# A hashed attention with a max-out network on one core: an earlier projection, a shorter run of zero products, and weights, quad projection and one hash at other units

## The chip, the cores and the metric

The kernel runs on one core of one Trainium2 chip. The metric is device time in microseconds, the median of several executions. TensorE is called PE in the profile, VectorE DVE, ScalarE ACT, GpSimd POOL, and SyncE SP. PE's weight loads are listed apart as PEld.

## The reference

Two stages follow each other. Only the first output feeds the second:

```python
# q, k, v: (4, 8, 768, 64) float32; proj: (64, 6)
q_bits = (einsum('bhsd,dk->bhsk', q, proj) > 0)      # 6 hash bits for each query
k_bits = (einsum('bhsd,dk->bhsk', k, proj) > 0)      # 6 hash bits for each key
mask   = bucket(q_bits)[..., :, None] == bucket(k_bits)[..., None, :]
scores = where(mask, q @ k.T / 8, -1e9)
attn   = softmax(scores)
x      = (attn @ v).transpose(0, 2, 1, 3).reshape(3072, 512)
h      = maximum(maximum(x @ w1, x @ w2), x @ w3)    # w1..w3: (512, 768)
out    = h @ w_out                                    # (768, 512)
```

## The kernel before

The hash bits are appended to the queries and keys as extra rows (plus and minus a half), so that one matrix product gives the scores and the comparison of the buckets together. A *unit* is one set of score products (L296, function `scores`), 768 score columns in all, followed by one exponential on ACT (L304) into an `AT` tile. There are 192 units, 48 for each of the four batches (`UPB`). The first batch is cut into chunks of 256 queries and the others into chunks of 384. Within the first three chunks the heads come in the order 0, 1, then 2 and 3, then 4 to 7; in later batches a batch's chunk runs through its eight heads, so that heads 4 to 7 of the second batch start at unit 60. `scores(u + 1)` is issued at the head of the loop body of unit `u`.

Queries and keys must stand with the 64 dimensions on the partitions. The first batch's heads 0 to 7 of both sides are grouped in *pairs* (0 to 3, two heads each). They are loaded in natural order (`load_pair`, L117), transposed on PE with the identity (`pair_turn`, L122), copied out of PSUM by DVE or ACT (`pair_keep`, L129 and L131), and narrowed into the tile `S` by POOL (`pair_place`, L136). The bits are products with the small projection `pj2` (L149, L169), compared with zero by DVE (L152, L174). The other batches are grouped in *quads* of four heads (`g` from 2 to 7, `g = 3` being heads 4 to 7 of the second batch): loaded by SP or POOL (`load_quad`, L194), transposed in blocks on DVE (`turn`, L200), narrowed by POOL (`narrow`, L205), placed into `S` by DMAs of SP (`place`, L210), and hashed by `quad_hash`: eight pairs of PE products with the quad projection `pj` (L219), one comparison on DVE (L222), and four DMAs of SP that put the bits into `S` (L230).

The order on every engine is the order of the program text (a manual schedule). Before the loop stand the first loads, a run of products of the tile `warm`, which is zero (L498), and the first pair's transposes, hash and placement. Both projections come from the same small tile `pst`, the projection matrix loaded by one DMA (L478): `pj2` is filled by two copies on DVE and two on POOL (L493), `pj` by a memset and four copies on POOL (L534, L536). The values come by `load_v` (L238) and the weights of the network by `load_weights` (L246, and L243 for the output weights), all through POOL's queue.

Other steps are attached to units by `when(u, f)`: they run in the body of unit `u`, behind `scores(u + 1)`. Then come one or two groups of the network (`ffn_groups`: L406 products, L411, L413 or L415 evacuation; L450 products and L454 copy for the output), then the *burst* of a finished set of four heads, if one is due (`burst`: sums of the exponentials, L351, and values, L373). A quad's hash is the last thing in its unit, and its four DMAs are put at the head of the next:

```python
            if u in hash_at:
                when(u + 1, quad_hash(hash_at[u]))
```

The PSUM banks other than those of the scores are four, given out and returned in program order.

Of the kernel before, what the change touches and what calls it, by code (L numbers as in the profile page):

```python
# [17 lines left out]
def kernel(  # L18
# [12 lines left out]
    nc = tc.nc  # L31
    B, H, S, D = q.shape
    NBITS = proj.shape[1]
# [7 lines left out]
    Q = 32  # L41
# [35 lines left out]
    pj = konst.tile([P, 2, Q], FP32, name="pj")  # L77
    pj2 = konst.tile([P, Q], FP32, name="pj2")
    pst = konst.tile([Q, 2, NBITS], FP32, name="pst")
# [10 lines left out]
    def bank():  # L90
        i = free_banks.pop(0)
        return i, bank_tiles[i]
# [7 lines left out]
    def start_set(name, heads):  # L100
        nat[name] = nat_pool.tile([P, 4 * NM * D], FP32, tag="nat", name="nat")
        for x, key in enumerate(heads):
            where[key] = (name, x)
# [7 lines left out]
    def load_pair(pi, eng, sides=(1, 0), h0=0, h1=2):  # L111
        if pi not in nat:
            start_set(pi, [(0, 2 * pi), (0, 2 * pi + 1), (1, 2 * pi), (1, 2 * pi + 1)])
        n = nat[pi].rearrange("p (s h w) -> p s h w", s=2, h=2)
        for side in sides:
            src = (q, k)[side][0, 2 * pi + h0 : 2 * pi + h1].rearrange("h (p c) d -> p h (c d)", p=P)
            eng.dma_start(n[:, side, h0:h1, :], src)  # L117
# [15 lines left out]
    def pair_place(pi, side, par, h0=0, h1=2):  # L133
        o = s_tile(pi)[0:D, 2 * side + h0 : 2 * side + h1, par * HALF : (par + 1) * HALF]
        i_ = t32[pi][par * D : (par + 1) * D, side, h0 * HALF : h1 * HALF].rearrange("d (h n) -> d h n", n=HALF)
        nc.gpsimd.tensor_scalar(out=o, in0=i_, scalar1=RS, scalar2=1.0, op0=AluOp.mult, op1=AluOp.mult)  # L136
# [98 lines left out]
    def load_v(g):  # L235
        b, h0 = divmod(4 * g, H)
        t = v_at[g] = vo_pool.tile([P, 4, NM * D], FP16, tag="vo", name="vo")
        nc.gpsimd.dma_start(t[:], v[b, h0 : h0 + 4].rearrange("h (p c) d -> p h (c d)", p=P))  # L238


    def load_weights(i):
        if i == 3:
            nc.gpsimd.dma_start(wout_sb[:], moe_w_out.rearrange("(c p) f -> p c f", p=P))  # L243
            return
        w = (moe_w1, moe_w2, moe_w3)[i]
        nc.gpsimd.dma_start(w_sb[i].rearrange("p (i u) f -> p i (u f)", u=2),  # L246
                            w.rearrange("(i p u) f -> p i (u f)", p=P, u=2))
# [224 lines left out]
    def when(u, f, *args):  # L472
        at.setdefault(u, []).append(lambda: f(*args))

    with tc.manual_schedule():
        load_pair(0, nc.sync, (1,), 0, 1)
        load_pair(0, nc.scalar, (0,), 0, 1)
        nc.sync.dma_start(pst[:], proj.rearrange("(u d) k -> d u k", d=Q))  # L478
        nc.vector.memset(warm[:], 0.0)
        make_identity(nc, iden[:])  # L480
        load_pair(0, nc.sync, (1,), 1, 2)
# [9 lines left out]
        for hd in range(2):  # L491
            for u in range(2):
                (nc.vector, nc.gpsimd)[hd].tensor_copy(  # L493
                    pj2[hd * D + u * Q : hd * D + (u + 1) * Q, hd : hd + 2 * NBITS - 1 : 2], pst[:, u, :])
        load_v(0)
        iw, wp = bank()
        for n in range(11):
            nc.tensor.matmul(wp[:, 0:HALF], warm[:, 0:P], warm[:], start=True, stop=True)  # L498
        give(iw)

# [30 lines left out]
        for side in (1, 0):  # L531
            for par in range(2):
                pair_place(0, side, par, 1, 2)
        nc.gpsimd.memset(pj[:], 0.0)  # L534
        for x in range(4):
            nc.gpsimd.tensor_copy(pj[x * Q : (x + 1) * Q, :, x : x + 4 * NBITS - 3 : 4], pst[:])  # L536

        for pi, us in ((1, ((0, 1, 0), (0, 0, 0), (3, 1, 1), (4, 0, 1))), (2, ((6, 1, 0), (7, 1, 1), (9, 0, 0), (10, 0, 1))),
                       (3, ((11, 1, 0), (13, 1, 1), (14, 0, 0), (15, 0, 1)))):
            for u, side, hd in us:  # L540
                when(u, pair_group, pi, side, hd, nc.scalar if pi == 1 and hd == 1 else None)
                if pi == 1:
                    for par in range(2):
                        when(u, pair_place, pi, side, par, hd, hd + 1)
                elif hd == 1:
                    for par in range(2):
                        when(u, pair_place, pi, side, par)
# [7 lines left out]
        when(18, pair_hash, 3)  # L555
        when(19, t32.pop, 3)
        when(17, load_v, 1)
        for n, u in ((0, 3), (1, 12), (2, 21), (3, 31)):
            when(u, load_weights, n)
        when(13, load_quad, 0, 2, range(4), nc.gpsimd)  # L560
        for u, side, g in ((23, 1, 3), (27, 0, 3)):
# [1 line left out]
        hash_at = {}  # L563
        for g in range(2, NQUAD):
            b2, i2 = divmod(g, 2)
            need = UPB * b2 + 12 * i2
            for n, side in enumerate((1, 0)):
                name = (side, g)
                if g > 3:
                    us = [SPREAD[b2][0] + SPREAD[b2][1] * (8 * i2 + 4 * n + n2) // 4 for n2 in range(4)]  # L570
                    for x in range(4):
                        when(us[0] - 14 + x, load_quad, side, g, (x,), nc.gpsimd)
                else:
                    us = [need - {2: 26, 3: 23}[g] + 4 * n + n2 for n2 in range(4)]
                for n2, u2 in enumerate(us):
                    when(u2, turn, name, n2 // 2, n2 % 2)
                    if n2 % 2:
                        when(u2 + 1, narrow, name, n2 // 2)
                when(us[3] + 3, place, name, range(4))
            hash_at[{2: 32, 3: 48, 4: need - 12}.get(g, need - 9)] = g  # L580
            when({2: 36, 3: 46}.get(g, need - 22), load_v, g)

        ffn, credit = [], 0
# [2 lines left out]
        for c, i in sorted(done_at, key=lambda e: done_at[e]):  # L586
            d = done_at[c, i] + LAG[c > 2]
            sums, values = burst(c, i)
            pieces = [lambda f=sums: f(0, NM), lambda f=values: f(0, 0, NM), lambda f=values: f(1, 0, NM)]
            for n, f in enumerate(pieces):  # L590
                u = {(0, 0): (16, 17, 20), (1, 0): (21, 22, 24), (2, 0): (26, 27, 29)}.get((c, i), (d, d, d))[n]
# [67 lines left out]
```

## Time and profile before

| | |
|---|---|
| median of 3 runs | 268.19 us (267.94 to 268.28) |
| the profiled execution's own time | 268.58 us |
| its span, first to last instruction | 266.6 us |
| PE busy | 257.9 us (97%) |
| DVE busy | 208.9 us (78%) |
| ACT busy | 177.3 us (67%) |
| POOL busy | 69.9 us (26%) |
| DMA | 30.95 MB, mean 116 GB/s |

The times of the rows of a trace count from the start of the span. The profiled execution is one execution, 0.39 us above the median of the others, and 1.98 us of its time lie outside its span. In rows of the timeline, the first number is the start, the second the duration, and `x3` says that three instructions are merged in the row. Bracketed is the idle time of the engine ahead of the row and what ended it, as far as the profile can tell. SPq, ACTq and PEldq are the queues that issue. The pages name a tile by the name that the program gave it, and both projections `pj` and `pj2` go by `pj` there.

### The profile page before, as it was taken

What the parts mean: (1) busy time and instruction counts of PE and PEld (TensorE: products, weight loads), DVE (VectorE), ACT (ScalarE), POOL (GpSimd) and SP (SyncE); (2) the same over time, 40 slices, a digit from 0 to 9 for tenths busy, and PEclk for the clock granted to TensorE, in tenths of its full rate; (3) what the DMA queues carried; (4) which work ended last, traced back from release to release, by engine and by line L of the source; (5) the groups of instructions that cost most, each with busy time, mean ns of one, the idle gap of its engine ahead of it and who ended that gap; (6) DMA issues with size and microseconds to landing.
All of it is one profiled execution on the core that took longest, in us unless ns stands there. A gap on an engine that the chain in (4) does not pass through costs nothing.

```text
span 266.6 us, 6482 instructions
## 1 busy us (share of the span) xinstructions
PE 257.9 (97%) x2505; PEld 154.4 (58%) x2505; DVE 208.9 (78%) x493; ACT 177.3 (67%) x257; POOL 69.9 (26%) x132
## 2 busy tenths in 40 slices
PE   7899999999799999999999999999999999999995
PEld 4555557885566575555555554555555555554552
DVE  2897685987499999978998997899849785888361
ACT  3596785676758694984869578484895859581322
POOL 3588652355032535240141612011000000000000
PEclk9999999999999999999999999999999999999999
DMA  6977999969703791982054472802030003000303
GB/s 203 316 156 135 230 234 212 245 114 233 185 22 86 159 231 18 234 222 53 4 167 131 56 182 43 204 8 61 15 118 4 0 2 119 2 0 2 118 0 118
DMA packets 20717, 30.95 MB, mean 116 GB/s; under 512 B 2608, under 2 KB 15248, under 8 KB 20688
## 3 DMA queue, kind: packets, MB, share of 16 engines
q0 software_dynamic: 8128, 13.37, 26.6%
q1 hardware_dynamic: 12128, 16.66, 21.8%
q10 hardware_dynamic: 432, 0.52, 0.6%
q8 instruction: 19, 0.31, 0.5%
q14 instruction: 10, 0.08, 0.1%
HBM read 25.17 MB, written 6.29 MB: 118 GB/s over the span
## 4 chain that ended last, share of the span: by engine, by line
PE 84%; DVE 7%; ACT 5%; issue 3%; DVEq 0%; ACTq 0%
PE ms L406 31%; PE sc L296 21%; PE ms L373 11%; PE ms L450 10%; ACT AT L304 4%; PE ms L351 3%; PE ms L219 3%; DVE ht L415 2%; DVE ad L327 1%; PE ms L498 1%; PE ms L122 1%; PE ms L149 1%; DVE T L131 1%; PE ms L169 1%; DVE S L174 1%
## 5 line engine op out<-in xcount | busy, mean ns | idle before, releaser
L304 ACT ACTIVATE AT<-sc 128x768 f16<-128x768 f32 x192 | 152.3, 816 | 62.2 <-PE sc L296 60.7
L406 PE MATMUL ms<-xT,w_sb 128*128 128x384 f16 (+1 forms) x648 | 114.8, 307 | 0.1
L296 PE MATMUL sc<-S 72*128 72x384 bf16 (+1 forms) x432 | 93.6, 308 | 3.3 <-ACT AT L304 1.8
L406 PEld LDWEIGHTS <-w_sb 128*128 128x128 f16 x648 | 62.7, 97 | 35.9 <-issue 0.4
L415 DVE TENSOR_TENSOR ht<-ht,ms 128x384 f16<-128x384 f16 (+1 forms) x108 | 54.3, 504 | 24.4 <-PE ms L406 13.4
L296 PEld LDWEIGHTS <-S 72*128 72x128 bf16 (+1 forms) x432 | 39.4, 98 | 35.7 <-issue 15.5
L205 POOL TENSOR_SCALAR T<-T 128x768 bf16<-128x768 f32 x24 | 22.8, 952 | 95.4 <-issue 50.5
L450 PE MATMUL ms<-wout_sb,ht 128*128 128x512 f16 x138 | 35.5, 378 | 0.0
L373 PE MATMUL ms<-AT,vo 128*32 128x385 f16 (+3 forms) x864 | 35.2, 309 | 0.3 <-DVE ht L415 0.3
L327 DVE TENSOR_TENSOR ad<-ad,AT 128x768 f16<-128x768 f16 x48 | 26.6, 553 | 2.1 <-ACT AT L304 1.3
L373 PEld LDWEIGHTS <-vo 128*32 128x32 f16 x864 | 22.6, 96 | 9.6 <-issue 1.8
L200 DVE STREAM_TRANSPOSE T<-nat 128x384 f32<-128x384 f32 x48 | 27.0, 565 | 0.2 <-DMA nat<-in_q_dram 0.2
L327 DVE TENSOR_TENSOR ad<-AT,AT 128x768 f16<-128x768 f16 x48 | 26.2, 546 | 0.2 <-ACT AT L304 0.2
L411 ACT CAST ht<-ms 128x384 f16<-128x384 f32 x36 | 17.3, 479 | 8.1 <-PE ms L406 8.1
L380 DVE SCALAR_TENSOR_TENSOR xT<-ms,sv,rb 128x384 f16<-128x384 f32 (+1 forms) x36 | 19.8, 567 | 1.4
L450 PEld LDWEIGHTS <-ht 128*128 128x128 f16 x138 | 13.3, 97 | 13.0 <-issue 0.3
L454 ACT COPY osb<-ms 128x512 f32<-128x512 f32 x21 | 12.2, 585 | 8.2 <-PE ms L450 6.3
L330 DVE TENSOR_TENSOR ad<-ad 128x384 f16<-128x384 f16 x32 | 15.5, 484 | 1.1
L136 POOL TENSOR_SCALAR S<-T 64x384 bf16<-64x384 f32 (+1 forms) x23 | 14.2, 617 | 5.0 <-DVE T L131 3.5
L358 DVE STREAM_TRANSPOSE ys<-ms 128x384 f32<-128x384 f32 (+1 forms) x18 | 9.6, 532 | 6.2 <-PE ms L351 6.2
L194 POOL DMA_DIRECT2D nat<-in_q_dram x20 | 11.1, 560 | 0.1
L413 DVE CAST ht<-ms 128x256 f16<-128x256 f32 x18 | 7.4, 413 | 4.0 <-PE ms L406 3.9
(48 smaller groups left out, 123.0 us busy)
## 6 DMA issues: line engine op xcount, KB each, us to landing
out_dram<-osb SPq DMA_DIRECT2D x21, 256.0 KB
S<-T SPq DMA_DIRECT2D x48, 96.0 KB
nat<-in_q_dram POOLq DMA_DIRECT2D x20, 192.0 KB, 6.7
vo<-in_v_dram POOLq DMA_DIRECT2D x8, 384.0 KB, 6.2
nat<-in_k_dram POOLq DMA_DIRECT2D x16, 192.0 KB, 5.7
w_sb<-in_moe_w_dram POOLq DMA_DIRECT2D x3, 768.0 KB, 6.9
nat<-in_k_dram SPq DMA_DIRECT2D x10, 192.0 KB
nat<-in_k_dram SPq DMA_DIRECT2D x3, 384.0 KB
```

The source lines that it names most:

```text
L200: nc.vector.transpose(t32[name][:, u, half * HALF : (half + 1) * HALF], i_)
L205: nc.gpsimd.tensor_scalar(out=t16[name][:, u, :], in0=t32[name][:, u, :], scalar1=RS, scalar2=1.0, op0=AluOp.mult, op1=AluOp.mult)
L296: nc.tensor.matmul(views[j], s_of[kn][0 : D + bits, kx, m * P : (m + 1) * P], s_of[qn][0 : D + bits, qx, q0 : q0 + w], start=True, stop=True)
L304: nc.scalar.activation(t[:, :, 0:w], whole, ActFn.Exp, bias=-SCALE * 0.25 * bits, scale=SCALE)
L327: nc.vector.tensor_tensor(out=sum_of[c, h][:], in0=t[0], in1=t[n], op=AluOp.add)
L330: nc.vector.tensor_tensor(out=t[:, 0, :], in0=t[:, 0, :], in1=t[:, 1, :], op=AluOp.add)
L373: nc.tensor.matmul(av[Q * x : Q * (x + 1), 0:n], v_at[2 * b + i][:, x, cb * D + side : (cb + 1) * D : 2], weights_of(c, 4 * i + x, m)[:, 0 ...
L380: nc.vector.scalar_tensor_tensor(out=xt_of(c)[:, 2 * i + side, 0:w], in0=av[:, 0:w], scalar=sv_of[b, i, side][:], in1=rb[0][:, 0:w], op0=A ...
L406: nc.tensor.matmul(ps[:, 0:w], w_sb[wi][:, jc, fb * P : (fb + 1) * P], xt[:, jc, 0:w], start=(jc == 0), stop=(jc == NJC - 1))
L411: nc.scalar.copy(hts[fb][:, 0:w], ps[:, 0:w])
L415: nc.vector.tensor_tensor(out=hts[fb][:, 0:w], in0=hts[fb][:, 0:w], in1=ps[:, 0:w], op=AluOp.max)
L450: nc.tensor.matmul(ps[:, 0:DM], hts[fb][:, tb * P : (tb + 1) * P], wout_sb[:, fb, :], start=(fb == 0), stop=(fb == NFB - 1))
```

## The change

The projection's load moves from SP's queue to the head of ACT's queue, ahead of the first queries. The run of zero products is cut from eleven to nine. The first weight is issued right behind the first values, ahead of the loop, instead of at unit 3; the second at unit 9 instead of 12, the third at unit 20 instead of 21. The quad projection `pj` is filled at unit 19 instead of ahead of the loop. The hash of quad 3 is put at unit 47 instead of 48.

```diff
     with tc.manual_schedule():
         load_pair(0, nc.sync, (1,), 0, 1)
+        nc.scalar.dma_start(pst[:], proj.rearrange("(u d) k -> d u k", d=Q))
         load_pair(0, nc.scalar, (0,), 0, 1)
-        nc.sync.dma_start(pst[:], proj.rearrange("(u d) k -> d u k", d=Q))
...
         load_v(0)
+        load_weights(0)
         iw, wp = bank()
-        for n in range(11):
+        for n in range(9):
             nc.tensor.matmul(wp[:, 0:HALF], warm[:, 0:P], warm[:], start=True, stop=True)
...
-        nc.gpsimd.memset(pj[:], 0.0)
-        for x in range(4):
-            nc.gpsimd.tensor_copy(pj[x * Q : (x + 1) * Q, :, x : x + 4 * NBITS - 3 : 4], pst[:])
-
+        def fill_pj():
+            nc.gpsimd.memset(pj[:], 0.0)
+            for x in range(4):
+                nc.gpsimd.tensor_copy(pj[x * Q : (x + 1) * Q, :, x : x + 4 * NBITS - 3 : 4], pst[:])
+
+        when(19, fill_pj)
...
-        for n, u in ((0, 3), (1, 12), (2, 21), (3, 31)):
+        for n, u in ((1, 9), (2, 20), (3, 31)):
             when(u, load_weights, n)
...
-            hash_at[{2: 32, 3: 48, 4: need - 12}.get(g, need - 9)] = g
+            hash_at[{2: 32, 3: 47, 4: need - 12}.get(g, need - 9)] = g
```

## The prediction

> **What bounds the kernel now.** First the head of the page: busy time by engine and the chain that ended last.
>
> ```profile
> span 266.6 us, 6482 instructions
> PE 257.9 (97%) x2505; PEld 154.4 (58%) x2505; DVE 208.9 (78%) x493; ACT 177.3 (67%) x257; POOL 69.9 (26%) x132
> PE 84%; DVE 7%; ACT 5%; issue 3%; DVEq 0%; ACTq 0%
> ```
>
> TensorE (PE) is busy for 257.9 of 266.6 us and carries 84% of the chain. So the time is the sum of PE's work plus its gaps, 8.7 us in all, and a change gains what it takes out of either, if nothing late takes its place. I then read the timeline where PE is not dense. The first place is the start. Columns: start, duration, engine, line, operation; in brackets the idle time before it and what ended it.
>
> ```profile
> 0.74 0.89 ACTq L117 DMA_DIRECT2D nat<-in_q_dram  x2
> 1.13 3.70 PE L498 MATMUL ms<-warm 128*128 128x384 f16 x11 [1.13 <-DVE pj L487]
> 1.19 0.42 SPq L478 DMA_DIRECT2D pst<-in_proj_dram  x1
> 4.01 0.37 SPq L117 DMA_DIRECT2D nat<-in_q_dram  x1
> 4.29 0.34 DVE L493 COPY pj<-pst 32x6 f32<-32x6 f32 x2 [2.68 <-DMA pst<-in_proj_dram]
> 4.62 1.10 PE L122 MATMUL ms<-iden,nat 128*128 128x128 f32 x6
> 4.95 0.95 POOL L238 DMA_DIRECT2D vo<-in_v_dram  x1 [0.18 <-issue]
> 5.44 0.56 DVE L131 COPY T<-ms 128x384 f32<-128x384 f32 x1 [0.81 <-PE ms L122]
> 6.05 1.44 PE L169 MATMUL ms<-T,pj 128*6 128x384 f32 x8 [0.32 <-DVE T L131]
> 6.09 1.57 POOL L136 TENSOR_SCALAR S<-T 64x384 bf16<-64x384 f32 x3 [0.20 <-DVE T L131]
> 6.90 2.31 DVE L174 TENSOR_SCALAR S<-ms 6x384 bf16<-6x384 f32 x4 [0.90 <-PE ms L169]
> 8.08 0.49 PE L296 MATMUL sc<-S 70*128 70x256 bf16 x3 [0.60 <-DVE S L174]
> 9.09 1.48 PE L122 MATMUL ms<-iden,nat 128*128 128x128 f32 x12
> ```
>
> The first transposes (L122, 4.62) show no wait: they stand behind eleven products of zeros (L498), and all after them is a chain: T copy on DVE (5.44), hash on PE (6.05), bits on DVE (6.90), first scores (8.08). Whoever starts the transposes earlier moves that chain.
>
> The second place is one unit of the scores, far behind the start:
>
> ```profile
> 56.67 0.60 PE L406 MATMUL ms<-xT,w_sb 128*128 128x256 f16 x4
> 57.10 0.49 PE L296 MATMUL sc<-S 72*128 72x384 bf16 x2
> 59.95 1.46 PE L219 MATMUL ms<-T,pj 128*32 128x384 f32 x16
> 61.49 0.56 DVE L222 TENSOR_SCALAR bits<-ms 128x384 bf16<-128x384 f32 x1 [0.28 <-PE ms L219]
> 53.29 6.18 SPq L210 DMA_DIRECT2D S<-T  x8
> 62.08 2.94 SPq L230 DMA_DIRECT2D S<-bits  x4
> 69.54 0.49 PE L296 MATMUL sc<-S 72*128 72x384 bf16 x2
> 69.87 0.60 PE L406 MATMUL ms<-xT,w_sb 128*128 128x256 f16 x4
> 71.95 0.48 PE L296 MATMUL sc<-S 72*128 72x384 bf16 x2 [1.48 <-ACT AT L304]
> 72.91 0.42 DVE L415 TENSOR_TENSOR ht<-ht,ms 128x256 f16<-128x256 f16 x1 [1.89 <-PE ms L406]
> L304 ACT ACTIVATE AT<-sc x60: 804/811/854, 8.6 to 70.1; 128x768 f16<-128x768 f32 x60
> PE sc L296 <- ACT AT L304: 1.5, 1, 1.5
> ```
>
> PE stands still for 1.48 us before the scores at 71.95. The last two lines are the instructions of L304 up to 71.9 us (count, then nanoseconds) and the waits of PE between 60 and 84 us. Sixty units had been activated by then, so the scores that wait are unit 60's: the first of heads 4 to 7 of the second batch (48 units a batch, 12 for the first four heads), the quad g = 3. The profile names ACT as releaser, but the last activation started at 70.1 and took 0.81, so it was done at 70.95, a whole microsecond earlier. What unit 60 alone needs are the hash bits of quad 3. They are hashed at 59.95, written by DVE until 62.05, sent by SP in four DMAs from 62.08 to 65.02. Busy time and DMA load by stretch (the last three columns are PE clock, DMA share, GB/s):
>
> ```profile
> 58.00:72.00 14.00, 12.52 (x150) 8.07 (x150) 8.75 (x21) 9.17 (x13) 4.44 (x16) 1.00 1.03 212
> 72.00:74.00 2.00, 2.00 (x16) 1.49 (x17) 1.09 (x3) 1.47 (x2) 0.00 (x0) 1.00 0.06 14
> ```
>
> The DMA engines are full from 58 on (share 1.03) and nearly empty right after 72 (0.06): the bits came with the last of that load. For comparison, quad 2's four sends and the scores that use them, which did not wait:
>
> ```profile
> 48.37 2.96 SPq L230 DMA_DIRECT2D S<-bits  x4
> 56.34 0.49 PE L296 MATMUL sc<-S 72*128 72x384 bf16 x2
> ```
>
> There 7.97 us from the first send were enough; in quad 3's case 9.87 (62.08 to 71.95) passed.
>
> **The change, part by part.** *Two zero products fewer.* From the first of eleven to the transposes behind the last it is 4.62 - 1.13 = 3.49 us, so they are 0.32 apart, and two are 0.64. The transposes could start at 3.98. They also need the first keys. SP's issue at 4.01 is the seventh there; a wait of 0.4 us stands before it in the list of SP's waits:
>
> ```profile
> SPq L117 <- DMA nat<-in_q_dram: 0.4, 1, 0.4
> ```
>
> So the first queries had landed at about 4.0; of the keys, issued on SP ahead of the projection's 1.19, no row shows it. They are there by 4.62; nearest is the queries' 4.0. That bounds this gain by 0 and 0.64. I take 0.5, near the upper end, since the keys go out as early as the queries.
>
> *The projection ahead of the queries on ACT's queue.* One issue costs 0.42 (SP's row at 1.19). It leaves SP, whose later loads go out 0.45 earlier, and puts the queries back by 0.42, to 4.4. They are needed after the three transposes of the keys (half of 1.10 behind 4.0 to 4.1, so 4.55): hidden by 0.1; beyond that the bits of the queries, second in the row of four at 6.90, give another half microsecond of cover. The projection itself, issued at 0.74 for 1.19, lands about 0.45 earlier, 3.84 for 4.29, so its two DVE copies (0.34) are over at 4.2, ahead of the T copy due at 4.9. Cost nothing.
>
> *First weight behind the first values.* POOL now issues it ahead of three placements (6.09, 1.57). Its issue is 0.76:
>
> ```profile
> 17.06 0.76 POOL L246 DMA_DIRECT2D w_sb<-in_moe_w_dram  x1
> 12.68 0.93 POOL L536 COPY pj<-pst 32x12 f32<-32x12 f32 x4
> 33.66 0.82 POOL L205 TENSOR_SCALAR T<-T 128x768 bf16<-128x768 f32 x1 [2.50 <-DVE T L200]
> ```
>
> POOL's values issue ended at 5.90; 0.45 earlier that is 5.45, and with the weight 6.21. The placements then run 6.21 to 7.78, the first over at 6.73 against first scores due at 8.08 - 0.5 = 7.6. Hidden by 0.8. The 0.76 at 17.06 and the quad projection's copies at 12.68 leave a POOL that nobody waits for there; nothing gained. The quad projection at unit 19 is queued ahead of the narrowing at 33.66, where POOL idled 2.50: 0.93 and a memset fit. Second weight three units, third one unit earlier: nothing on the path.
>
> *Hash of quad 3 at unit 47 instead of 48.* It now stands behind the feed-forward group at 56.67, where the scores at 57.10 began, so 59.95 - 57.10 = 2.85 us earlier. PE's work is only reordered: the scores at 57.10 and the sums and values between them and 59.95 go back by the hash's 1.4 us and end where the hash ended. DVE's bits end 2.10 us after the hash starts (62.05 - 59.95), now at 59.2. On SP they stand behind the eight placements (53.29 + 6.18 = 59.47), so the first send goes at 59.5 for 62.08: 2.6 us earlier. If landing follows, unit 60's data are there at 71.92 - 2.6 = 69.3, and even at the 9.87 us of that crowded stretch at 69.4. PE would come to unit 60 one step of 0.77 after 69.54 (groups of scores and L406 stand at 69.54 and 69.87), at 70.31. So the wait goes with about 0.9 to spare. What it is worth: 1.48 (gap) to 1.64 (71.95 - 70.31); I take 1.48. Late next is ACT, done with unit 59 at 70.95 and needed by unit 61's scores at 71.1; then DVE, which had idled 1.89 for the same stall and so moves with PE.
>
> **Sum.** 0.5 + 1.48 = 1.98 us off the profiled execution's 268.58 gives 266.6; that execution was 0.39 above the median of 268.19. Against the median: 266.2.
>
> **The rivals.** (a) *The bits land earlier, but not enough.* They follow 8 placements in one SP queue while the DMA engines are full; half of the 2.6 us would put them at 70.6, leaving 0.3, a quarter at 71.3, leaving about 1. Time 266.5 to 267.2. Against it: those values' end, which POOL's next quad loads are queued behind, also comes 1.4 us later, so they press on the bits later. (b) *The stall is not the bits*, and stays: only 0.5 is won, 267.7. For it: no row names the DMA. Against it: quad 3's first unit is the one that waits, and 0.06 of DMA share right after.
>
> (c) *The clock opens later.* The products of zeros have 384 columns and go 0.32 apart; two scores of 384 columns fill 69.54 to 69.87, 0.165 each. So PE starts at half rate, though the granted clock reads 1.00 in every stretch. The six transposes at 4.62 take 0.18 each, the twelve at 9.09 take 0.12: the rate rose during the first ones. With nine products PE has done 0.64 less by then. Eight hash products at full rate:
>
> ```profile
> 11.15 0.83 PE L169 MATMUL ms<-T,pj 128*6 128x384 f32 x8
> ```
>
> If the clock opens one such stretch (some 4 us) later, the chain up to unit 1 runs two hash products (0.2), two units' scores (six of 256 columns, 0.11 each, 0.66) and three transposes (0.36) at half rate and loses about 1.2. Then 268.19 - 1.98 + 1.2 = 267.4.
>
> [...]
>
> (d) *The other side: the clock stays low until PE is dense*, past 12 us. From the first hash to there PE does 16 hash products (1.66), 15 scores (1.65) and 15 transposes (1.8), 5.1 us of work in the 6.4 from 6.05 to 12.4. At half rate (0.32 / 0.165 = 1.94) that is 9.9, so 3.5 us are lost and the time is 269.7, slower by 1.5. It eats the whole gain once 3.5 of the 5.1 us is done at half rate (1.94 x 3.5 - 3.5 - 1.3 of slack = 1.98), that is with an opening after about 12 us. Against it: PE works on with gaps of at most 0.6 us from 1.13, as before.
>
> (e) *The first weight takes DMA time from the pair loads.* The rate at the start:
>
> ```profile
> 0.00:12.00 12.00, 9.76 (x58) 5.44 (x59) 5.80 (x38) 4.72 (x7) 5.02 (x15) 1.00 0.88 258
> 12.00:16.00 4.00, 3.93 (x34) 2.51 (x35) 3.46 (x7) 3.99 (x7) 3.40 (x10) 1.00 1.13 252
> ```
>
> The four pairs (0.79 MB each) and the first values (0.79) are 3.94 MB; 3.1 are moved by 12 us, the rest at 252 GB/s by 15.3. The weight's 1.57 MB (512 x 768 x 4 bytes), all ahead of the last pair, cost 6.2 us more: 21.5. That pair's first transposes:
>
> ```profile
> 19.19 0.49 PE L122 MATMUL ms<-iden,nat 128*128 128x128 f32 x3
> ```
>
> Due at 18.7 after the gain at the start, they would wait 2.8 us: 269.0. It turns the sign where the pair lands 1.98 us late, at 20.7. Against it: the weight is queued behind the values, which are themselves in flight till 15.
>
> **How the numbers follow.** Forecast 0.73; (a) 0.08, (b) 0.05, (c) 0.06, (d) 0.05, (e) 0.03. Faster by over 0.2% (0.54 us, about what a measurement tells): forecast, (a), (c), 0.87; within: (b), 0.05; slower: (d), (e), 0.08. The range runs from both gains at their ends, 0.64 + 1.64 = 2.28, and 0.2 for the scatter of the runs below, 265.7, to (a) and (c) above, 267.4.
>
> **What would show it.** Right: L498 x9, first transposes at 4.0 to 4.2, first scores at 7.5 to 7.7; hash L219 at 56.6, sends from about 59, no gap over 0.3 before the sixty-first activation. Wrong: transposes that wait for nat, hash products twice as long as 0.83 for eight, or unit 60 still waiting beside sends that left 2.6 us earlier.

## The result, and the profile after

| | before | after |
|---|---|---|
| median | 268.24 us (267.94 to 268.51, 4 runs) | 266.78 us (266.3 to 266.83, 4 runs) |
| the profiled execution's own time | 268.58 us | 266.3 us |
| its span | 266.6 us | 264.2 us |

The ratio of the times is 0.9937, with a 95% interval of 0.9919 to 0.9956: the changed kernel is 0.4 to 0.8% faster. Forecast were 266.2 us, a ratio of 0.9926. The same kernel, run twice more beside other experiments, came to 0.9921 (0.9897 to 0.9945) and 0.9921 (0.9895 to 0.9946).

The head of the page of the changed kernel, and the groups' line of the scores (busy time and mean ns, then idle time in front of them and its main cause):

```profile
span 264.2 us, 6478 instructions
PE 257.7 (98%) x2503; PEld 154.1 (58%) x2503; DVE 208.6 (79%) x493; ACT 177.5 (67%) x257; POOL 70.1 (27%) x132
PE 87%; DVE 6%; issue 2%; ACT 1%; DMA 1%; POOL 1%; ACTq 0%; DVEq 0%
L296 PE MATMUL sc<-S 72*128 72x384 bf16 (+1 forms) x432 | 93.6, 308 | 1.3 <-DVE S L174 0.5
```

PE's busy time moved by 0.2 us only (257.9 to 257.7); what went is idle time. ACT's part of the chain fell from 5% to 1%, and the scores no longer name ACT as their main releaser. The timeline of the changed kernel at the start, read in the chain's order:

```profile
0.74 0.42 ACTq L477 DMA_DIRECT2D pst<-in_proj_dram  x1
1.13 3.06 PE L499 MATMUL ms<-warm 128*128 128x384 f16 x9 [1.13 <-DVE pj L487]
3.98 1.63 PE L122 MATMUL ms<-iden,nat 128*128 128x128 f32 x6
4.95 0.42 PEld L122 LDWEIGHTS ms<-iden,nat 128*128 128x128 f32 x3 [0.52 <-DMA nat<-in_q_dram]
5.54 1.83 PE L169 MATMUL ms<-T,pj 128*6 128x384 f32 x8
6.39 2.36 DVE L174 TENSOR_SCALAR S<-ms 6x384 bf16<-6x384 f32 x4 [0.96 <-PE ms L169]
7.62 0.49 PE L296 MATMUL sc<-S 70*128 70x256 bf16 x3 [0.26 <-DVE S L174]
```

The transposes start behind nine products, at 3.98 for 4.62. The first scores stand at 7.62 for 8.08, 0.46 earlier. One pair of profiles says little here, since this start scatters: over all the profiles of the runs, the first scores stand at 8.08 to 8.29 in the four with the old start and at 7.36 to 7.94 in the six with the start of the change. New is a wait on PE's weight loads: the queries' transposes (the last three of six) waited 0.52 us for their data. And at the place of the stall of unit 60:

```profile
56.48 1.50 PE L219 MATMUL ms<-T,pj 128*32 128x384 f32 x16
57.91 0.50 PE L296 MATMUL sc<-S 72*128 72x384 bf16 x2
58.63 2.94 SPq L230 DMA_DIRECT2D S<-bits  x4
61.91 1.10 POOL L194 DMA_DIRECT2D nat<-in_k_dram  x2 [0.40 <-issue]
62.99 2.19 POOL L194 DMA_DIRECT2D nat<-in_q_dram  x4
67.44 5.33 ACT L304 ACTIVATE AT<-sc 128x768 f16<-128x768 f32 x7
69.83 0.49 PE L296 MATMUL sc<-S 72*128 72x384 bf16 x2
```

The hash runs ahead of the scores of a unit (57.91), the bits are sent at 58.63 for 62.08, and the scores of unit 60 (69.83) have no bracket, that is no idle time before them; ACT's seven activations, unit 60's among them, follow each other without a break.

### The profile page after: what moved, and what is told of

It reads as the page before. It is cut to its first block, busy times and chain, and to the rows that moved or that the text cites. A ratio compares the mean times of both kernels' runs of the same rounds, so it can differ in the third digit from the quotient of the medians.

```text
span 264.2 us, 6478 instructions
## 1 busy us (share of the span) xinstructions
PE 257.7 (98%) x2503; PEld 154.1 (58%) x2503; DVE 208.6 (79%) x493; ACT 177.5 (67%) x257; POOL 70.1 (27%) x132
## 4 chain that ended last, share of the span: by engine, by line
PE 87%; DVE 6%; issue 2%; ACT 1%; DMA 1%; POOL 1%; ACTq 0%; DVEq 0%
PE ms L406 33%; PE sc L296 22%; PE ms L373 11%; PE ms L450 11%; PE ms L219 3%; PE ms L351 3%; PE ms L122 2%; DVE ht L415 2%; DVE ad L327 1%; ACT AT L304 1%; DMA nat<-in_q_dram 1%; DVE S L174 1%; PE ms L169 1%; PE ms L149 1%; POOL S L136 1%
## 5 line engine op out<-in xcount | busy, mean ns | idle before, releaser
L406 PE MATMUL ms<-xT,w_sb 128*128 128x384 f16 (+1 forms) x648 | 114.8, 307 | 0.1
L406 PEld LDWEIGHTS <-w_sb 128*128 128x128 f16 x648 | 62.7, 97 | 36.0 <-issue 0.4
L174 DVE TENSOR_SCALAR S<-ms 6x384 bf16<-6x384 f32 x16 | 8.9, 554 | 2.2 <-PE ms L169 1.8
```

The lines of the kernel that those rows point to most:

```text
L406: nc.tensor.matmul(ps[:, 0:w], w_sb[wi][:, jc, fb * P : (fb + 1) * P], xt[:, jc, 0:w], start=(jc == 0), stop=(jc == NJC - 1))
```

## The experiments

The theory was the prediction's: 0.5 us from the two zero products, 1.48 from the bits that come in time, nothing from the rest. Its main rivals: the stall at unit 60 is not the bits; the weights or the projection cost or win something; PE's rate rises later with fewer products.

**The parts alone.** First the one number of the hash, in the kernel before:

```diff
-            hash_at[{2: 32, 3: 48, 4: need - 12}.get(g, need - 9)] = g
+            hash_at[{2: 32, 3: 47, 4: need - 12}.get(g, need - 9)] = g
```

> The kernel before with one edit: quad 3 hashed at unit 47. Theory A (the stall at unit 60 is the landing of quad 3's bits, and the start is a second, separate gain): the gap of 1.48 us before unit 60 goes, 1.4 to 1.7 us faster, some 266.6. Theory B (the gain of the whole change is the earlier weight traffic, which frees the DMA engines): the gap stays or shrinks by less than half, under 0.7 us faster.

Measured: 267.21 us beside 268.34, ratio 0.9952 (0.9935 to 0.9970), so 0.8 to 1.7 us. Its timeline has the hash, the sends and unit 60's scores so:

```profile
57.87 1.50 PE L219 MATMUL ms<-T,pj 128*32 128x384 f32 x16
60.02 2.94 SPq L230 DMA_DIRECT2D S<-bits  x4
71.22 0.49 PE L296 MATMUL sc<-S 72*128 72x384 bf16 x2
```

No idle time stands before unit 60. That the stall is something other than quad 3's hash is out. Unit 60 also needs quad 3's placements (L210); SP issued these at 53.96 to 59.82 here and at 53.29 to 59.47 before, so they were not what came late. And the DMA engines were still full here when unit 60 began (share 1.02 from 68 to 72 us): its data did not have to wait for the end of that load.

The start alone, in the kernel before:

```diff
+        nc.scalar.dma_start(pst[:], proj.rearrange("(u d) k -> d u k", d=Q))
         load_pair(0, nc.scalar, (0,), 0, 1)
-        nc.sync.dma_start(pst[:], proj.rearrange("(u d) k -> d u k", d=Q))
...
-        for n in range(11):
+        for n in range(9):
```

> The kernel before with two edits: the projection ahead of the first queries on ACT's queue, and nine zero products. Theory A: first scores 0.46 us earlier as in the changed kernel, the gap before unit 60 stays, 0.4 to 0.5 us faster, some 267.75. Theory B: under 0.2 us, since the gap absorbs what the start wins.

Measured: 267.82 us, ratio 0.9985 (0.9963 to 1.0007): 0.4 us, and not told from nothing by the time alone. By its timeline the first scores are 0.57 earlier than before's, and unit 60 still waits:

```profile
7.51 0.49 PE L296 MATMUL sc<-S 70*128 70x256 bf16 x3 [0.42 <-DVE S L174]
71.56 0.48 PE L296 MATMUL sc<-S 72*128 72x384 bf16 x2 [1.44 <-ACT AT L304]
```

The weights and the quad projection alone, in the kernel before:

```diff
         load_v(0)
+        load_weights(0)
...
-        nc.gpsimd.memset(pj[:], 0.0)
...
+        when(19, fill_pj)
...
-        for n, u in ((0, 3), (1, 12), (2, 21), (3, 31)):
+        for n, u in ((1, 9), (2, 20), (3, 31)):
```

> The kernel before with the third group of edits alone: first weight behind the first values, second at unit 9, third at unit 20, quad projection filled at unit 19. Theory A: nothing on the path, within 0.2 us of the kernel before, first scores 8.1 and gap at unit 60 as before. Theory B: 0.3 us or more faster, with a smaller gap, or less waiting of ACT between 36 and 48 us, where the changed kernel's trace was 0.25 us ahead.

Measured: 268.08 us, ratio 0.9990 (0.9973 to 1.0007): nothing that can be measured, and the stall remains.

```profile
71.82 0.48 PE L296 MATMUL sc<-S 72*128 72x384 bf16 x2 [1.18 <-ACT AT L304]
```

The whole change on the same chip:

> The changed kernel itself once more, on the chip of the three parts. Theory A: its gain is the sum of the first two parts, 1.9 to 2.1 us, some 266.3. The first comparison had 1.5 by the medians and 2.3 by the two profiled executions; if the medians are right the sum of the parts is more than the whole and something takes 0.4 back.

Measured: 266.33 us, ratio 0.9921. By the medians the three parts sum to 1.13 + 0.52 + 0.26 = 1.9 us, the whole is 2.0; the last two are not told from nothing each by itself. Its start shows what the first profile only began to:

```profile
4.42 0.56 DVE L131 COPY T<-ms 128x384 f32<-128x384 f32 x1 [0.91 <-PE ms L122]
5.33 0.31 PEld L122 LDWEIGHTS ms<-iden,nat 128*128 128x128 f32 x3 [1.19 <-DMA nat<-in_q_dram]
5.34 0.55 PE L122 MATMUL ms<-iden,nat 128*128 128x128 f32 x3 [0.95 <-DMA nat<-in_q_dram]
5.81 1.83 PE L169 MATMUL ms<-T,pj 128*6 128x384 f32 x8
7.90 0.49 PE L296 MATMUL sc<-S 70*128 70x256 bf16 x3 [0.26 <-DVE S L174]
```

The keys were transposed and copied out by 4.98, yet their hash begins at 5.81: it stands on PE behind the queries' transposes, which waited till 5.34.

Last, the hash put back in the changed kernel:

```diff
-            hash_at[{2: 32, 3: 47, 4: need - 12}.get(g, need - 9)] = g
+            hash_at[{2: 32, 3: 48, 4: need - 12}.get(g, need - 9)] = g
```

> The changed kernel with one part undone: the hash of quad 3 back at unit 48. Theory A (the gap ahead of unit 60 is the bits' lateness, and only the earlier hash takes it away in the changed kernel): the sends go out at about 61.6 us, POOL's loads of quad 4 lie beside them, and a gap of 1.2 to 1.5 us returns ahead of the sixty-first activation; the start stays as in the changed kernel; 267.7 us on the median, 267.2 to 268.0, some 1.3 us more than the changed kernel. Theory B (the earlier weights have changed the traffic enough): no gap over 0.5 us and 266.3 to 266.9 us.

Measured: 267.44 us, ratio 0.9969 (0.9951 to 0.9986); the changed kernel's three medians are 266.33 to 266.78, so the hash is worth 0.7 to 1.1 us there. The gap is back, beside the same start and the same weights:

```profile
61.61 2.94 SPq L230 DMA_DIRECT2D S<-bits  x4
71.32 0.48 PE L296 MATMUL sc<-S 72*128 72x384 bf16 x2 [1.32 <-ACT AT L304]
```

**Early sends, or quad loads out of the way?** The change sends the bits earlier, and by that also ahead of most of POOL's loads of quad 4, which went out at 61.91 and 62.99 in the profile after. In the timeline of before they stand around the first send at 62.08:

```profile
61.09 1.09 POOL L194 DMA_DIRECT2D nat<-in_k_dram  x2 [0.40 <-issue]
62.17 2.18 POOL L194 DMA_DIRECT2D nat<-in_q_dram  x4
```

Two runs take the two apart. The first leaves the hash at 48 and takes quad 4's loads from POOL, putting them behind the bits in SP's queue:

```diff
-                        when(us[0] - 14 + x, load_quad, side, g, (x,), nc.gpsimd)
+                        when(us[0] - (11 if g == 4 else 14) + x, load_quad, side, g, (x,), nc.sync if g == 4 else nc.gpsimd)
```

> The kernel before, quad 3 still hashed at unit 48, but quad 4's eight loads are issued by SP behind the bits of quad 3 instead of by POOL ahead of them. Theory A (the bits are late because POOL's quad loads share the DMA engines while the bits are under way): with the sends still at about 62, the bits land by 69 and the gap before unit 60 is gone or under 0.4 us; 1.1 to 1.5 us faster than before. Theory B (what counts is the moment of the sends, and landing follows it by nearly ten microseconds): the gap of 1.48 stays, within 0.3 us of before.

Measured: 266.8 us beside 268.4, ratio 0.9942 (0.9914 to 0.9971).

```profile
62.29 2.94 SPq L230 DMA_DIRECT2D S<-bits  x4
65.27 1.87 SPq L194 DMA_DIRECT2D nat<-in_k_dram  x4
70.52 0.49 PE L296 MATMUL sc<-S 72*128 72x384 bf16 x2
64.00:68.00 4.00, 4.00 (x24) 2.04 (x22) 2.02 (x5) 3.67 (x6) 0.00 (x0) 1.00 0.46 130
```

The bits left at 62.29, as late as before, and unit 60 (70.52) did not wait. From 64 to 68 us the DMA engines were 46% busy. So 8.2 us from the send are enough when POOL's loads are not beside the bits.

The second leaves the early hash and moves quad 4's loads ahead, to units 44 to 47, so that they are under way when the bits go:

```diff
-                        when(us[0] - 14 + x, load_quad, side, g, (x,), nc.gpsimd)
+                        when(44 + x if g == 4 else us[0] - 14 + x, load_quad, side, g, (x,), nc.gpsimd)
```

> The changed kernel, except that the eight loads of quad 4 go out on POOL two a unit at units 44 to 47, ahead of the sums' and values' end that they are queued behind now, so that they are under way when the bits of quad 3 are sent. The hash and the sends stay where the change put them. Theory A (the early send alone is enough): the loads move before or beside the bits, but the bits have 9 us or more from the first send to unit 60; no gap there over 0.3 us, and the time of the changed kernel, 266.3 to 266.8 us. Theory B (what decides is which quad loads lie beside the bits): the bits sent at about 59 arrive late again; a gap of 0.5 to 1.5 us returns ahead of the sixty-first activation, and the time is 266.8 to 268.0 us. Also possible: the sends themselves are unhindered, since the loads are over by 63 us.

Measured: 266.85 us, ratio 0.9941 (0.9923 to 0.9959), beside 266.4 for the changed kernel on the same chip.

```profile
58.90 0.58 POOL L194 DMA_DIRECT2D nat<-in_q_dram  x1
59.02 2.94 SPq L230 DMA_DIRECT2D S<-bits  x4
69.71 0.49 PE L296 MATMUL sc<-S 72*128 72x384 bf16 x2
56.00:60.00 4.00, 4.00 (x77) 2.36 (x79) 1.97 (x5) 1.71 (x3) 3.94 (x8) 1.00 0.97 226
```

The loads go out right up to and beside the first sends, the DMA engines are full (0.97 from 56 to 60 us), and unit 60 still has no gap: 10.7 us from the send are enough under load. The loads were also over sooner here (a share of 0.39 from 68 to 72 us, 0.91 before); in the run with the hash alone they were not (1.02), and there 11.2 us from the send were enough. So with the sends left late, moving the loads removes the stall, and with the loads beside the bits, sending earlier removes it; the change has both, since the earlier hash also puts most of the loads back (63.29 for 61.09 in the run with the hash alone). A run with the early sends and the loads exactly where they were was not made. Beside the loads the bits needed 9.57 to 9.87 us from the send to the scores in the four profiles that had the gap; without them at most 8.23, in the first of these two runs. So the loads cost the bits at least 1.3 us. By what step the loads hold up the bits, no row here shows.

**The start.** The projection behind the first queries on ACT's queue, in the changed kernel:

```diff
-        nc.scalar.dma_start(pst[:], proj.rearrange("(u d) k -> d u k", d=Q))
         load_pair(0, nc.scalar, (0,), 0, 1)
+        nc.scalar.dma_start(pst[:], proj.rearrange("(u d) k -> d u k", d=Q))
```

> The changed kernel with the projection behind the first queries on ACT's queue instead of ahead of them. Theory A (in the changed kernel the queries land 0.4 late, and the hash of the keys, which stands behind the queries' transposes on PE, pays for it): no wait for the queries before their transposes, first scores 0.2 to 0.4 us earlier than in the changed kernel, 0.2 to 0.4 us faster than it. Theory B (the queries' delay is hidden by the bits of the keys): the same time as the changed kernel within 0.15 us, or 0.2 slower since the projection is late for the copies.

Measured: 266.52 us, ratio 0.9927 (0.9902 to 0.9952); the changed kernel has 0.9921 to 0.9937. The queries are not waited for, the projection's copies are 1.26 later (4.49 for 3.23), and the first scores stand at 7.52: no difference that can be measured.

```profile
3.98 1.45 PE L122 MATMUL ms<-iden,nat 128*128 128x128 f32 x6
4.49 0.33 DVE L493 COPY pj<-pst 32x6 f32<-32x6 f32 x2 [2.88 <-DMA pst<-in_proj_dram]
7.52 0.49 PE L296 MATMUL sc<-S 70*128 70x256 bf16 x3 [0.33 <-DVE S L174]
```

No zero products at all, in the changed kernel (the loop of L498 removed):

> The changed kernel with no product of zeros at all. Theory A (the clock opens only after some 4 us of work): transposes at about 3.7 to 4, but the clock opens 3 us or more later than 5.2, the first hash and scores run at half rate, first scores near 8.5 to 9.5, 0.7 to 2 us slower than the changed kernel. Theory B (the products do nothing but hold the transposes back): transposes and all behind them no later than in the changed kernel, the same time.

Measured: 267.18 us, ratio 0.9954 (0.9922 to 0.9986), about 0.8 over the 266.4 that the changed kernel has on the same chip (the last run below, 0.9895 to 0.9946). The intervals overlap, and the ten executions without the products lie between 266.51 and 269.25, so the time alone does not settle it. The trace is clearer:

```profile
3.51 0.88 PE L122 MATMUL ms<-iden,nat 128*128 128x128 f32 x3 [3.51 <-DMA nat<-in_k_dram]
5.99 2.46 PE L169 MATMUL ms<-T,pj 128*6 128x384 f32 x8
8.71 1.21 PE L296 MATMUL sc<-S 70*128 70x256 bf16 x6 [0.26 <-DVE S L174]
```

The first keys are there at 3.51, so nine zero products put the transposes back by 0.47 us. But without them eight hash products take 2.46 us, where the same count takes 0.83 at 10.70 in the profile after, and the first scores come 1.1 us later than in the profile after. By this trace the zero products are worth their time.

Thirteen transposes of the identity in place of the nine products, in the changed kernel, to see whether the hash behind them runs as fast as behind the products:

```diff
-        for n in range(9):
-            nc.tensor.matmul(wp[:, 0:HALF], warm[:, 0:P], warm[:], start=True, stop=True)
+        for n in range(13):
+            nc.tensor.transpose(wp[:, 0:P], iden[:], iden[:])
```

> The changed kernel with thirteen transposes of the identity in place of the nine products of zeros, which fill about the same 2.8 us. [...]

Measured: 266.69 us, ratio 0.9934 (0.9911 to 0.9957), as the changed kernel.

```profile
1.36 3.04 PE L499 MATMUL ms<-iden 128*128 128x128 f32 x13 [1.36 <-POOL iden masks.py:199]
5.69 1.70 PE L169 MATMUL ms<-T,pj 128*6 128x384 f32 x8
7.73 0.49 PE L296 MATMUL sc<-S 70*128 70x256 bf16 x3 [0.34 <-DVE S L174]
```

The hash runs as fast as behind nine products (1.44 to 1.83 in the profiles that have them), not as without any (2.46).

Last, an attempt to go further, seven products and the projection behind the queries, and the changed kernel beside it:

```diff
-        for n in range(9):
+        for n in range(7):
```

> The changed kernel with the projection behind the first queries on ACT's queue (as in the earlier run with it there) and seven zero products instead of nine. Theory A (the start is bounded by the zero products and the landing of the first keys, which came at 3.5 us in the run without zero products): transposes at about 3.5 us, first scores at 7.1 to 7.3 instead of 7.6, 0.3 to 0.4 us faster than the changed kernel: 266.0 us on the median, 265.9 to 266.4. Theory B (fewer products let the clock open later): the opening comes later than 6 us, the first hash takes over 2 us, and what the transposes win is given back: 266.3 to 266.9 us. A difference under 0.5 us may not show against the scatter of the runs.

> The changed kernel once more, on the same chip as the two runs beside it, to compare them with: 266.3 to 266.8 us, first scores at 7.6 to 7.9, no gap over 0.3 us ahead of the sixty-first activation.

Measured: 266.51 us, ratio 0.9932 (0.9905 to 0.9959), and 266.4 us for the changed kernel. First seven products, then nine:

```profile
1.13 2.42 PE L499 MATMUL ms<-warm 128*128 128x384 f16 x7 [1.13 <-DVE pj L487]
3.84 1.28 PE L122 MATMUL ms<-iden,nat 128*128 128x128 f32 x6 [0.29 <-DMA nat<-in_k_dram]
5.50 1.37 PE L169 MATMUL ms<-T,pj 128*6 128x384 f32 x8 [0.39 <-DVE T L131]
7.54 0.49 PE L296 MATMUL sc<-S 70*128 70x256 bf16 x3 [0.67 <-DVE S L174]
```

```profile
3.98 1.49 PE L122 MATMUL ms<-iden,nat 128*128 128x128 f32 x6
7.94 0.49 PE L296 MATMUL sc<-S 70*128 70x256 bf16 x3 [0.71 <-DVE S L174]
```

With seven the transposes wait for the keys and start only 0.14 earlier. So the transposes are at their bound, the landing of the first keys, and no version was measurably faster than the changed kernel.

## Why the prediction was right, step by step

**Two zero products fewer: right, at the size.** Taken was 0.5, with 0.64 as the upper bound. The transposes did start the full 0.64 earlier, and the first scores 0.46. Where the missing 0.2 went is not settled: the queries were late (the next point), and PE was slower in that execution, with 1.83 us for the eight hash products instead of 1.44. The second alone can do it: in the last profile of the changed kernel nothing waited for the queries, the hash products took 1.75 us, and the first scores were only 0.14 earlier than before. The bound that no row then showed, the landing of the first keys, is 3.5 to 3.8 us by the runs with none and with seven products.

**The projection "cost nothing": this step failed.** It put the queries' landing at 4.4, hidden by 0.1, and said that the bits of the queries gave another half microsecond of cover. Their weight loads waited for them till 4.95 and 5.33 in the two profiles above (4.78 in the run of the start alone, 5.16 in that without zero products), and that cover does not exist: in the program the keys' hash stands behind the queries' transposes, and the rows of the second profile show it waiting there. The cost was 0.95 us of idle PE in one execution; in three other profiles of the same start (the runs with the hash put back, with the early loads, and the last of the changed kernel) no weight load waited for the queries. Why they come late in some executions only stays open. The cost is small beside the scatter: putting the projection behind the queries made no difference that the medians tell. The projection itself gained more than was forecast: its copies on DVE stand at 3.23 for 4.29, 1.06 earlier instead of 0.45.

**Weights and quad projection: nothing, as said.** Alone they gave a ratio of 0.9990 (0.9973 to 1.0007). That also removes the rival in which the first weight holds up the pair loads and the time rises to 269.0.

**The hash of quad 3: right.** Forecast were the hash at 56.6 (56.48 came), the sends from about 59 (58.63) and no gap at unit 60 (none). The cause, bits held up by the DMA load beside them, was inferred and is now shown from both sides: the stall goes when the bits leave earlier beside the loads, and it goes when they leave as late as before and the loads are moved. The 1.48 lies in the upper part of what was measured: on medians the hash is worth 1.13 alone (0.8 to 1.7) and 0.7 to 1.1 when undone. The gap itself was 1.18 to 1.48 us in four executions that had it, and its largest stood in the profile that the prediction was made from.

**The rivals.** That the stall is not the bits is out. That PE's rate rises later by a stretch of 4 us did not happen: eight hash products took 1.37 to 1.83 us in all runs with seven or nine products, against 2.46 with none. The 4 us were the author's estimate, and no run with seven or nine products shows such a delay; with none the first two scores, at 8.71, took 0.59 us, where two took 0.38 at 8.88 in the profile before. The price of 1.2 us put on it was of the right kind: about 0.8 by the medians when the products were all taken away. A rate that stays low past 12 us is out too: at 10.70 in the profile after, eight hash products took 0.83 us.

**The sum.** 1.98 was forecast; the profiled pair differs by 2.28, the medians by 1.46 beside the first comparison and by 2.0 and 1.9 in the two later ones. That the forecast comes so near to the two later pairs is in part luck: the hash alone was worth less than 1.48 by the medians, the start scatters by as much as it wins, and the profiled pair holds something that no step spoke of. ACT paused 0.28 us at one activation before, and not after.

```profile
46.38 3.73 ACT L304 ACTIVATE AT<-sc 128x768 f16<-128x768 f32 x5 [0.28 <-ACT AT L304]
```

```profile
43.35 6.04 ACT L304 ACTIVATE AT<-sc 128x768 f16<-128x768 f32 x8 [3.01 <-PE sc L296]
```

The pause stands in all four profiles with the old start, the run of the weights alone and that of the hash alone among them, and in none of the ten with a changed start; in the former PE's next scores start 0.24 later behind the products of the network (L406). Its cause was not tested and stays open.

## What to carry to other kernels

When one unit stalls and an engine is named that had long been done, compare what only that unit needs, and look at the DMA load just before and just after the stall; then test the cause from both sides, the late data sent earlier and the competing load moved. In this kernel a small transfer that shared the DMA engines with large loads had to be sent with more lead than it needed without them, 9.6 to 9.9 us against at most 8.2. Cover that lies later in the data flow is no cover if the program puts the instruction that would use it behind the late one on the same engine: here the keys were copied out by 4.98 and hashed at 5.81, behind the queries' transposes, which had waited till 5.34.

## What the runs showed of the hardware

In this kernel transposes took the place of the zero products in bringing PE to its higher rate. With thirteen of them in the products' place eight hash products took 1.70 us, behind nine products 1.44 to 1.83, with neither 2.46. These were float32 transposes of 128 columns, which the trace lists as MATMUL. They themselves ran at the slow rate still (13 in 3.04 us, 0.23 each, against 0.12 later: 12 in 1.47 us at 8.74); the rate rose during the hash. Behind seven products, which filled 2.42 us where nine fill 3.06, the hash took 1.37 us.

The moment at which the rate rises differed between executions of the same instructions. These two rows are the first transposes of two kernels that have the same instructions up to there, the change with the hash put back and the changed kernel once more; the second was quoted above:

```profile
3.98 1.02 PE L122 MATMUL ms<-iden,nat 128*128 128x128 f32 x6
7.36 0.49 PE L296 MATMUL sc<-S 70*128 70x256 bf16 x3 [0.60 <-DVE S L174]
```

Six transposes took 1.02 us here and 1.49 there, the eight hash products 1.44 and 1.75, and the first scores stand at 7.36 and 7.94. This scatter of 0.58 us is as large as the gain of the two products. What sets the moment, no row shows. The granted clock reads 1.00 from 0 to 4 and from 4 to 8 us in the seven profiles read in such stretches, before and the run without zero products among them, so only the durations tell the rate.
